# Batch 6's second column maximum, the store and reading back of its maxima and the load of its a, sooner in a pinned order

## The chip, the cores and the metric

The kernel runs on one core of one Trainium2 chip. The metric is device time in microseconds; the figure of a kernel is the median of its runs, and lower is better.

## What is computed

Slot attention over 8 batches and 8 heads (576 positions, head size 64, 32 slots), then a feed-forward block with GELU on the 4608 rows of 512 that come out of it.

```python
a = phi - np.max(phi, axis=2, keepdims=True)
a = np.exp(a)
a = a / (np.sum(a, axis=2, keepdims=True) + 1e-09)
k_m = np.einsum('bhsm,bhsd->bhmd', a, k)
v_m = np.einsum('bhsm,bhsd->bhmd', a, v)
scores = scale * np.matmul(q, k_m.transpose(0, 1, 3, 2))
...
attn = np.exp(scores)
...
attn = np.matmul(attn, v_m)
...
h = x @ w_in
g = 0.5 * h * (1.0 + erf(h * inv_sqrt2))
return (g @ w_out)
```

The softmax of `phi` runs over the 576 positions, one maximum for each of the 8 x 32 columns of a batch.

## The kernel before

The work is cut into batches 0 to 7. For each batch the kernel makes `a` (from `phi`), pools `k` and `v` with it into 32 slots per head, takes scores of `q` against the slots, and multiplies the attention with `U`, which holds the slots already multiplied with `w_in`. So TensorE does per batch: `h` (line 901, attention times `U`), GELU on ScalarE, and the product with `w_out` (line 941). Each float32 product is made of three products of high and low parts: `gh` and `gl` are the two parts of the GELU's result.

A piece of work is named in a string, START, as `name.batch.part`, and the pieces are recorded in the order in which they stand there. Every engine, and SyncE's queue of transfers, then takes its own instructions strictly in that order. Pieces after the string's end are put by a second, planned list that is the same in both kernels. Near the end of START batch 3 is in its feed-forward steps and batches 5 and 6 are being prepared. Names that matter here:

- `h.3.x.0`, `gelu.3.x.0`, `gh.3.0.i`, `gl.3.0.i`, `P.3.0.i`: batch 3, first half of the positions: `h` for block x of 128 hidden columns, its GELU (lines 913 and 915), the high part and the low part for blocks 2i and 2i+1 (lines 244 and 928), and their 12 products with `w_out` (line 941). The steps `h.3.14.0` to `P.3.0.7` and the second half `h.3.x.1` come from the planned list.
- `Lphi.6.g`, `amax.6.g`, `mw.6`, `mr.6`: batch 6's `phi`, transposed, in two halves g; the negated maximum of each half's columns, on VectorE (line 426, into `nm`); the store of these maxima to a small buffer in DRAM (`row<-nm`, line 480); and their reading back, spread over all partitions (`cols<-row`, line 485).
- `Lphin.6`: the load of batch 6's `phi` in its other layout into the tile `aT` (lines 468 and 473). `aadd.6`: VectorE subtracts the maxima there (lines 516 and 520, `aT<-aT,cols`). `ax.6`: ScalarE's exponential of it (line 509). `aexp.6.g`: the exponential of the transposed half with its sum (line 432). The tiles `aT`, `cols` and `phi` have one buffer each.
- `slots.5`, `slots.6`: TensorE's pooling (lines 536 and 549), which reads `aT` and the `kv` tiles. `km.5`: the scaled result (line 581). `Lkv.6.g.c`: the ten loads of batch 6's k and v. `Lq.4`: three loads of q for batch 4, read by `score.4` (line 619, `psc<-q,kT`). `Lphi.7`: the next `phi`, into the same buffer.

`aadd.6` stands between `gl.3.0.5` and `gh.3.0.6` on VectorE, and `aexp.6`, `ax.6` between the GELUs of blocks 13 and 14 on ScalarE; both come from the planned list.

```python
def a_out(b):
    row = st["row", b] = dram.tile([P, G], F32, tag="row", name=f"row_{b}")
    nc.sync.dma_start(row, col("nm", b))
```

Of the kernel before, what the change touches and what calls it, by code (L numbers as in the profile page):

```python
# [137 lines left out]
h.3.0.0 gh.2.1.6 gelu.2.15.1 gl.2.1.6 h.3.1.0 P.2.1.5 P.2.1.6 gh.2.1.7:a gelu.3.1.0 gelu.3.0.0  # L138
h.3.2.0 gh.3.0.0 gl.2.1.7 h.3.3.0 gl.3.0.0 gelu.3.2.0 slotsT.4 Up.3.12.4 kT.4 gelu.3.3.0
Up.3.8.4 P.2.1.7 O.2.1.0:a h.3.4.0 O.2.1.1 Uh.3.12 P.3.0.0 Lkv.5.0.0 Uh.3.8 gh.3.0.1:a  # L140
gelu.3.4.0 gl.3.0.1 h.3.5.0 amax.6.0 h.3.6.0 gelu.3.5.0 gh.3.0.2:a h.3.7.0 gl.3.0.2 P.3.0.1
gelu.3.7.0 Ul.3.8 gelu.3.6.0 h.3.8.0 h.3.9.0 gelu.3.8.0 gh.3.0.3:a P.3.0.2 gl.3.0.3 aadd.5
pT.3.1 P.3.0.3 ax.5 amax.6.1 gelu.3.9.0 gh.3.0.4 slots.5.0 ph.3.1:d slots.5.1 Lkv.6.1.1
Lkv.6.1.4 km.5.0 Lkv.6.0.0 pl.3.1 Lkv.6.0.4 gl.3.0.4 Lphin.6 Ul.3.12 Lkv.6.0.2 mw.6 km.5.1
mr.6 Lkv.6.0.1 Lkv.6.1.3 Lkv.6.0.3 Lkv.6.1.2 Lkv.6.1.0
"""


# [1126 lines left out]
```

## Time and profile before

| | |
|---|---|
| median of 3 runs | 709.08 us (708.46 to 712.72) |
| profiled execution | 708.37 us |
| its span | 706.6 us |
| TensorE matmul busy | 686.3 us, 97% of the span |
| VectorE busy | 372.2 us, 53% |
| ScalarE busy | 306.2 us, 43% |
| mean granted TensorE clock | 0.985 |

The span is what the profiler's rows cover; 1.8 us of the execution's own time lie around it. Times in rows are microseconds from the span's start. PE is TensorE's matmul, DVE VectorE, ACT ScalarE, SPq SyncE's queue of transfers.

### The profile page before, as it was taken

To read this page: it belongs to the slowest core of one execution; us is meant where nothing else is said; L and a number is where in the kernel's file an instruction comes from. 1 tells how busy PE (TensorE), PEld (TensorE's weight loads), DVE (VectorE), ACT (ScalarE), POOL (GpSimd) and SP (SyncE) were. 2 spreads that over 40 slices of the span, in tenths; PEclk is the share of its full clock that TensorE was granted. 3 is DMA by queue.
4 is the path that set the end of the run, shared out by engine and by line. 5 is a ranking of instruction groups with operands and counts; after the bars stand their busy time and mean duration, and the time that the engine had idled before them with its cause. 6 is when DMAs were issued, how large, how long until landed. Compare 5 with 4: busy or idle time off the path is not lost.

```text
span 706.6 us, 12344 instructions
## 1 busy us (share of the span) xinstructions
PE 686.3 (97%) x4942; PEld 569.4 (81%) x4942; DVE 372.2 (53%) x689; ACT 306.2 (43%) x789; POOL 45.2 (6%) x38
## 2 busy tenths in 40 slices
PE   6799999999999999997999999999999999999997
PEld 5577888888768888885887888888887888788886
DVE  3989878855672634243944346432834346432222
ACT  5879668345452373443543225322521315322220
POOL 1333143300000000000000000000000000000000
PEclk9799999999999999998999999999999999999999
DMA  9973255412248161135600200020000200000001
GB/s 335 375 271 120 94 214 134 156 56 85 98 135 227 60 163 62 45 95 183 205 0 31 83 2 31 1 97 1 31 1 31 83 1 31 1 31 0 31 1 45
DMA packets 30717, 64.37 MB, mean 91 GB/s; under 512 B 3780, under 2 KB 8644, under 8 KB 30660
## 3 DMA queue, kind: packets, MB, share of 16 engines
q1 hardware_dynamic: 30564, 63.46, 26.9%
q8 instruction: 39, 0.64, 0.4%
q10 hardware_dynamic: 96, 0.13, 0.1%
q14 instruction: 18, 0.15, 0.1%
HBM read 54.13 MB, written 9.44 MB: 90 GB/s over the span
## 4 chain that ended last, share of the span: by engine, by line
PE 90%; DMA 6%; ACT 2%; DVE 1%; SPq 1%; issue 0%; POOL 0%; ACTq 0%
PE acc L941 49%; PE h L901 27%; PE tacc L941 6%; PE pu L619 4%; DMA raw<-w_out 2%; DMA raw<-w_in 1%; PE psc L619 1%; DMA kv<-kv 1%; PE psc L536 1%; DMA row<-nm 1%; DMA cols<-row 1%; PE x L536 1%; ACT phi L432 0%; PE pk L536 0%; SPq L288 0%
## 5 line engine op out<-in xcount | busy, mean ns | idle before, releaser
L941 PE MATMUL acc<-wo_hi,gh 128*128 128x512 f32 x512 | 202.0, 395 | 5.2 <-DVE gh L244 5.2
L901 PE MATMUL h<-p_hi,U 128*128 128x288 f32 x1024 | 201.6, 297 | 0.2 <-ACT tails L922 0.2
L941 PE MATMUL acc<-wo_hi,gl 128*128 128x512 f32 x512 | 200.3, 391 | 0.0
L941 PE MATMUL acc<-wo_lo,gh 128*128 128x512 f32 x512 | 200.3, 391 | 0.0
L913 ACT ACTIVATE gf<-h 128x256 f32<-128x256 f32 x192 | 73.8, 387 | 253.8 <-issue 158.4
L901 PEld LDWEIGHTS h<-p_hi,U 128*128 128x128 f32 x1024 | 162.7, 188 | 19.5 <-issue 7.5
L244 DVE CAST gh<-gf 128x512 fp32r<-128x512 f32 x100 | 42.4, 424 | 177.1 <-ACT gf L913 156.4
L941 PEld LDWEIGHTS acc<-wo_hi,gh 128*128 128x128 f32 x512 | 96.9, 189 | 29.6 <-DVE gh L244 5.4
L941 PEld LDWEIGHTS acc<-wo_hi,gl 128*128 128x128 f32 x512 | 96.5, 188 | 21.7 <-DVE gl L928 1.3
L928 DVE TENSOR_TENSOR gl<-gf,gh 128x512 fp32r<-128x512 f32 x128 | 90.3, 708 | 38.9 <-ACT gh L244 31.2
L941 PEld LDWEIGHTS acc<-wo_lo,gh 128*128 128x128 f32 x512 | 96.6, 189 | 16.2
L901 PE MATMUL h<-p_lo,U 128*128 128x288 f32 x512 | 108.7, 294 | 0.0
L901 PEld LDWEIGHTS h<-p_lo,U 128*128 128x128 f32 x512 | 81.3, 188 | 0.5 <-DVE p_lo L739 0.5
L860 DVE TENSOR_TENSOR U<-pu,U 128x512 fp32r<-128x512 f32 (+2 forms) x50 | 40.7, 835 | 30.8 <-ACT U L244 30.5
L915 ACT ACTIVATE tails<-h 128x32 f32<-128x32 f32 x192 | 37.5, 195 | 0.0
L619 PE MATMUL pu<-w_in_sb,kT 64*32 64x512 f32 (+2 forms) x624 | 34.4, 528 | 1.4 <-POOL w_in_sb L342 0.8
L244 ACT CAST U<-pu 128x512 fp32r<-128x512 f32 (+2 forms) x43 | 28.8, 710 | 7.4 <-PE pu L619 6.2
L941 PE MATMUL tacc<-wo_hi,gh_t 128*128 128x512 f32 x64 | 25.3, 395 | 0.0
L941 PE MATMUL tacc<-wo_lo,gh_t 128*128 128x512 f32 x64 | 24.9, 389 | 0.0
L941 PE MATMUL tacc<-wo_hi,gl_t 128*128 128x512 f32 x64 | 24.9, 389 | 0.0
L309 ACT ACTIVATE y<-raw 128x512 f32<-128x512 f32 x28 | 19.0, 680 | 8.0 <-DMA raw<-w_out 3.3
L342 POOL TENSOR_TENSOR y<-y,raw 128x512 int32<-128x512 int32 x14 | 18.8, 1343 | 57.7 <-DVE raw L318 25.3
(126 smaller groups left out, 576.5 us busy)
## 6 DMA issues: line engine op xcount, KB each, us to landing
kv<-kv SPq DMA_DIRECT2D x48, 256.0 KB, 5.3
out<-o SPq DMA_DIRECT2D x16, 512.0 KB, 2.9
raw<-w_out SPq DMA_DIRECT2D x14, 512.0 KB, 8.5
raw<-w_in SPq DMA_DIRECT2D x14, 512.0 KB, 4.9
q<-qT SPq DMA_DIRECT2D x9, 576.0 KB, 4.9
phi<-phiT SPq DMA_DIRECT2D x16, 288.0 KB, 4.7
aT<-phiN SPq DMA_DIRECT2D x6, 512.0 KB, 4.8
q<-qT SPq DMA_DIRECT2D x10, 288.0 KB, 7.7
```

Of the source, the lines that this page charges most:

```text
L244: return e.copy(dst, src) if e is nc.scalar else e.tensor_copy(dst, src)
L309: nc.scalar.activation(y, high.bitcast(F32), AF.Abs, scale=2.0**16)
L342: nc.gpsimd.tensor_tensor(w, y, low, op=ALU.add)
L536: nc.tensor.matmul(pk[32 * j : 32 * j + 32, : 2 * D], st["aT", b][:, c, g, 32 * j : 32 * j + 32], st["kv", b, g, c][:, :, j, :], start=(c ...
L619: nc.tensor.matmul(ps[g][M * j : M * j + M], st["kT", b][rows, t, M * j : M * j + M], moving[j][rows], start=True, stop=True,)
L860: nc.vector.tensor_sub(u[:, ..., 1, :], pu, u[:, ..., 0, :].bitcast(F32))
L901: i = nc.tensor.matmul(h[:, :HS], u[g][w], x[:, g, :], start=(n == 0), stop=(n == 3 * G - 1))
L913: nc.scalar.activation(gf[:, f % 2 * n : f % 2 * n + n], h[:, :n], AF.Gelu)
L915: nc.scalar.activation(t, h[:, n:HS], AF.Gelu)
L928: nc.vector.tensor_tensor(g_of("gl", *k), g_of("gf", *k), g_of("gh", *k).bitcast(F32), op=ALU.subtract)
L941: nc.tensor.matmul(acc, x, w[:, f, :], start=(first and n == 0), stop=(last and n == 2))
```

## The change

Three pieces of batch 6 move ahead in START, and nothing else does: `amax.6.1` and `mw.6` to right behind `amax.6.0`, `mr.6` to behind `ax.5`, and `Lphin.6` to ahead of `Lkv.6.1.1`. No instruction is added or taken away.

```diff
-gelu.3.4.0 gl.3.0.1 h.3.5.0 amax.6.0 h.3.6.0 gelu.3.5.0 gh.3.0.2:a h.3.7.0 gl.3.0.2 P.3.0.1
...
+gelu.3.4.0 gl.3.0.1 h.3.5.0 amax.6.0 amax.6.1 mw.6 h.3.6.0 gelu.3.5.0 gh.3.0.2:a h.3.7.0
...
+gl.3.0.3 aadd.5 pT.3.1 P.3.0.3 ax.5 mr.6 gelu.3.9.0 gh.3.0.4 slots.5.0 ph.3.1:d slots.5.1
+Lphin.6 Lkv.6.1.1 Lkv.6.1.4 km.5.0 Lkv.6.0.0 pl.3.1 Lkv.6.0.4 gl.3.0.4 Ul.3.12 Lkv.6.0.2
```

On SyncE's queue, around the loads of batch 6 (`row` and `cols` are `mw.6` and `mr.6`, `aT` is `Lphin.6`, `kv` and `kvw` are `Lkv.6`, the first line is a store of batch 2's output), the kernel before has:

```order
L980 DMA out<-o_1_3330 128x2x512
L382 DMA kv_0_0_3357<-kv 128x512
L382 DMA kv_1_1_3513<-kv 128x512
L372 DMA kvw_3515<-kv 64x512
L382 DMA kv_0_0_3519<-kv 128x512
L372 DMA kvw_3515<-kv 64x512
L468 DMA aT_3526<-phiN 128x4x256
L473 DMA aT_3526<-phiN 128x1x128
L382 DMA kv_0_2_3531<-kv 128x512
L480 DMA row_3533<-nm_3374 128x2
L485 DMA cols_3536<-row_3533 128x256
L382 DMA kv_0_1_3538<-kv 128x512
```

The same place of the queue in the changed kernel:

```order
L980 DMA out<-o_1_3330 128x2x512
L382 DMA kv_0_0_3357<-kv 128x512
L480 DMA row_3377<-nm_3374 128x2
L485 DMA cols_3468<-row_3377 128x256
L468 DMA aT_3517<-phiN 128x4x256
L473 DMA aT_3517<-phiN 128x1x128
L382 DMA kv_1_1_3520<-kv 128x512
L372 DMA kvw_3522<-kv 64x512
L382 DMA kv_0_0_3526<-kv 128x512
L372 DMA kvw_3522<-kv 64x512
L382 DMA kv_0_2_3535<-kv 128x512
L382 DMA kv_0_1_3538<-kv 128x512
```

The store and the reading back now stand ahead of all ten loads of batch 6, with the two `aT` loads right behind them; the five loads that stood ahead of the store stand behind.

On VectorE, from `gl.3.0.1` to `gh.3.0.4` (`nm` is the maximum, `aT` and `cols` here are batch 5's `aadd`), the kernel before has:

```order
L928 TENSOR_TENSOR gl_0_1_3365<-gf_0_1_3286,gh_0_1_3360 128x512
L426 TENSOR_REDUCE nm_3374<-phi_3021 128x1
L928 TENSOR_TENSOR gl_0_2_3394<-gf_0_2_3362,gh_0_2_3385 128x512
L860 TENSOR_TENSOR U_2_3317<-pu_8_3308,U_2_3317 128x2x512
L928 TENSOR_TENSOR gl_0_3_3445<-gf_0_3_3408,gh_0_3_3431 128x512
L516 TENSOR_TENSOR aT_3054<-aT_3054,cols_2950 128x1024
L520 TENSOR_TENSOR aT_3054<-aT_3054,cols_2950 64x128 x2
L802 STREAM_TRANSPOSE pT_1_3450<-sT_1_2751 128x576
L426 TENSOR_REDUCE nm_3374<-phi_3021 128x1
L244 CAST gh_0_4_3468<-gf_0_4_3428 128x512
```

And in the changed kernel:

```order
L928 TENSOR_TENSOR gl_0_1_3365<-gf_0_1_3286,gh_0_1_3360 128x512
L426 TENSOR_REDUCE nm_3374<-phi_3021 128x1 x2
L928 TENSOR_TENSOR gl_0_2_3397<-gf_0_2_3362,gh_0_2_3388 128x512
L860 TENSOR_TENSOR U_2_3317<-pu_8_3308,U_2_3317 128x2x512
L928 TENSOR_TENSOR gl_0_3_3448<-gf_0_3_3411,gh_0_3_3434 128x512
L516 TENSOR_TENSOR aT_3054<-aT_3054,cols_2950 128x1024
L520 TENSOR_TENSOR aT_3054<-aT_3054,cols_2950 64x128 x2
L802 STREAM_TRANSPOSE pT_1_3453<-sT_1_2751 128x576
L244 CAST gh_0_4_3472<-gf_0_4_3431 128x512
```

The second maximum has left its place behind batch 5's transpose and follows the first. The order on TensorE, ScalarE and GpSimd is the same in both kernels.

## Rows read from the trace of the kernel before

**Rows 1.** TensorE's waits from 60 us on: us in total, times, longest us.

```profile
PE acc L941 <- DVE gh L244: 5.2, 1, 5.2
PE h L901 <- ACT tails L922: 0.2, 1, 0.2
```

**Rows 2.** The chain that ended last, 283 to 345 us: start, us, what.

```profile
313.21 5.14 DMA row<-nm
...
318.37 5.04 DMA cols<-row
```

**Rows 3.** Timeline of SyncE's queue of transfers, 285 to 345 us: start, us, what.

```profile
293.26 16.41 SPq L382 DMA_DIRECT2D kv<-kv  x2
...
318.73 3.89 SPq L382 DMA_DIRECT2D kv<-kv  x5
322.67 0.43 SPq L413 DMA_DIRECT2D q<-qT  x1
...
324.16 1.03 SPq L358 DMA_DIRECT2D phi<-phiT  x2
```

**Rows 4.** VectorE's timeline; in brackets the idle time before, and what ended it.

```profile
295.84 0.75 DVE L426 TENSOR_REDUCE nm<-phi 128x1 f32<-128x576 f32 x1
297.58 0.69 DVE L928 TENSOR_TENSOR gl<-gf,gh 128x512 fp32r<-128x512 f32 x1 [0.99 <-ACT gh L244]
...
304.39 0.60 DVE L520 TENSOR_TENSOR aT<-aT,cols 64x128 f32<-64x128 f32 x2
...
305.72 0.71 DVE L426 TENSOR_REDUCE nm<-phi 128x1 f32<-128x576 f32 x1
...
323.43 1.23 DVE L516 TENSOR_TENSOR aT<-aT,cols 128x1024 f32<-128x1024 f32 x1 [9.09 <-DMA cols<-row]
...
325.19 0.43 DVE L244 CAST gh<-gf 128x512 fp32r<-128x512 f32 x1
...
330.60 1.47 DVE L426 TENSOR_REDUCE nm<-phi 128x1 f32<-128x576 f32 x2 [0.93 <-DMA phi<-phiT]
```

**Rows 5.** TensorE's timeline around the wait.

```profile
309.64 0.45 PE L549 MATMUL x<-kvw,aT 64*32 64x128 f32 x16
...
314.48 0.42 PE L901 MATMUL h<-p_hi,U 128*128 128x288 f32 x2
...
316.06 0.39 PE L941 MATMUL acc<-wo_hi,gh 128*128 128x512 f32 x1
...
318.77 0.42 PE L901 MATMUL h<-p_hi,U 128*128 128x288 f32 x2
...
325.67 0.80 PE L941 MATMUL acc<-wo_hi,gh 128*128 128x512 f32 x1 [5.16 <-DVE gh L244]
...
330.44 0.42 PE L901 MATMUL h<-p_hi,U 128*128 128x288 f32 x2
...
331.31 1.20 PE L619 MATMUL psc<-q,kT 64*32 64x288 f32 x32
```

**Rows 6.** Busy us by stretch, the last three: granted clock, DMA share, GB/s.

```profile
325.00:330.00 5.00, 4.33 (x11) 3.31 (x12) 2.64 (x7) 3.28 (x6) 0.00 (x0) 0.52 1.04 400
```

**Rows 7.** ScalarE's timeline from batch 6's exponentials on.

```profile
319.48 0.19 ACT L432 ACTIVATION_READ_ACCUMULATOR phi<-phi,nm 128x1 f32 x1
325.19 1.16 ACT L509 ACTIVATE aT<-aT 128x1152 f32<-128x1152 f32 x1 [5.52 <-DVE aT L520]
326.37 1.28 ACT L913 ACT_TABLE_LOAD   x1
327.67 0.38 ACT L913 ACTIVATE gf<-h 128x256 f32<-128x256 f32 x1
327.95 0.19 ACT L915 ACTIVATE tails<-h 128x32 f32<-128x32 f32 x1
```

**Rows 8.** The page's transfers: engine, count, KB each, median us from issue to landing.

```profile
q<-qT SPq DMA_DIRECT2D x9, 576.0 KB, 4.9
...
aT<-phiN SPq DMA_DIRECT2D x6, 512.0 KB, 4.8
q<-qT SPq DMA_DIRECT2D x10, 288.0 KB, 7.7
```

More of the change, by code (lines that the diff above doesn't have):

```diff
@@ L140 @@
 Up.3.8.4 P.2.1.7 O.2.1.0:a h.3.4.0 O.2.1.1 Uh.3.12 P.3.0.0 Lkv.5.0.0 Uh.3.8 gh.3.0.1:a
-gelu.3.4.0 gl.3.0.1 h.3.5.0 amax.6.0 h.3.6.0 gelu.3.5.0 gh.3.0.2:a h.3.7.0 gl.3.0.2 P.3.0.1
[L142 to L145, printed above, removed]
+gelu.3.4.0 gl.3.0.1 h.3.5.0 amax.6.0 amax.6.1 mw.6 h.3.6.0 gelu.3.5.0 gh.3.0.2:a h.3.7.0
+gl.3.0.2 P.3.0.1 gelu.3.7.0 Ul.3.8 gelu.3.6.0 h.3.8.0 h.3.9.0 gelu.3.8.0 gh.3.0.3:a P.3.0.2
+gl.3.0.3 aadd.5 pT.3.1 P.3.0.3 ax.5 mr.6 gelu.3.9.0 gh.3.0.4 slots.5.0 ph.3.1:d slots.5.1
+Lphin.6 Lkv.6.1.1 Lkv.6.1.4 km.5.0 Lkv.6.0.0 pl.3.1 Lkv.6.0.4 gl.3.0.4 Ul.3.12 Lkv.6.0.2
+km.5.1 Lkv.6.0.1 Lkv.6.1.3 Lkv.6.0.3 Lkv.6.1.2 Lkv.6.1.0
 """
```

## The prediction

> **What bounds the kernel now.** TensorE is busy for 97% of the span, so I first asked where it is not. The list of its waits from 60 us on has two rows, and only one is worth a step: 5.2 us, once, at the products with `w_out`, for VectorE's `gh` [rows 1]. Everything else on TensorE is work. TensorE's timeline puts that wait ahead of P.3.0.6, at 325.67 [rows 5]. Next I read the chain of waits backwards from there. It leaves TensorE for two transfers in a row, `row<-nm` (5.14 us from 313.21) and `cols<-row` (5.04 us from 318.37) [rows 2]. VectorE's timeline says the same from its side: it stood idle for 9.09 us before batch 6's `aadd` at 323.43, until `cols` had landed, and `gh`, queued behind it, could start only at 325.19 [rows 4]. So a small piece of batch 6's preparation holds up batch 3 because VectorE takes its work in order.
>
> Why was the store only issued at 313.21? Its data were there after 305.72 + 0.71 = 306.4 [rows 4]. SyncE's queue was blocked: the row of two loads that spans 16.41 us, from 293.26 to 309.67, is the last `kv` load of batch 5 and then the first of batch 6, which waits for the pooling of batch 5; and another six transfers stood between that one and `row` [rows 3].
>
> **What the wait costs.** A step runs `h`, products, `h`. In the step ahead, `h` to products is 316.06 - 314.48 = 1.58 us and products to the next `h` 318.77 - 316.06 = 2.71 [rows 5]. Without the wait P.3.0.6 would start at 318.77 + 1.58 = 320.35 and the next `h` at 323.06. That `h` started at 330.44 [rows 5], so the place costs 7.38 us: 5.32 of waiting and 330.44 - 325.67 - 2.71 = 2.06 because the 12 products ran slowly. The second part is TensorE's clock: the granted clock is 0.52 of full over 325 to 330, so nearly all of it at the lower of the two levels, 1.2 GHz, after 5 us in which TensorE did nothing [rows 6]. If the wait goes, both parts go.
>
> **The maxima, moved.** The first of batch 6's two maxima runs at 295.84 for 0.75 us; VectorE then sits idle for 0.99 us until 297.58, waiting for ScalarE [rows 4]. The second (0.71 us) fits into that gap and ends at about 297.3, so `gl.3.0.2` is not delayed. Cost nothing; without the gap it would be 0.7 us on VectorE alone. The other half of `phi` had to be there already: the first maximum shows no wait for it, and both halves were loaded together. The place left at 305.72 gives back 0.7 us of VectorE that nobody waits for.
>
> **The store and the reading back, moved.** On SyncE's queue `row` follows the last `kv` load of batch 5, issued at 293.26 [rows 3], so it goes out at about 297.3 and lands at 297.3 + 5.14 = 302.4. `cols` has one buffer, which batch 5's `aadd` reads until 304.39 + 0.60 = 305.0 [rows 4]; SyncE stands at it until then, and it lands at about 305.0 + 5.04 = 310.1. What is queued behind it on SyncE is `aT` and batch 6's `kv`; all of these wait for the pooling of batch 5, which ends at 309.64 + 0.45 = 310.1 [rows 5], or, for the first `kv` load, for a part of it that ended at about 309.2, so the new wait holds up nobody. It would start to when `row` took some 12 us instead of 5.
>
> **The load of a, moved.** It too has one buffer, free when that pooling ends: issue at 310.1, landing 4.8 us later [rows 8], 314.9. So `aadd.6` no longer waits for `cols` but for `aT`, from 314.9 on. It took 325.19 - 323.43 = 1.76 us up to `gh` [rows 4]: `gh.3.0.6` starts at about 316.7 and is done near 317.2, against 320.35 when TensorE wants it. Slack 3.2 us. Half of `kv` now stands behind `aT` and goes out about 2 us later than before, the other half sooner, as SyncE no longer stands at `cols` until 318.37 [rows 2].
>
> **What is late next.** TensorE comes 7.38 us sooner to everything behind the wait, and three things there do not all move as far.
>
> First, ScalarE. The `h` at 323.06 writes into a bank that the GELU of block 14 must have read. ScalarE ends `aexp.6` at 319.48 + 0.19 = 319.67 in both kernels; then come `ax.6`, a table load and that GELU, whose last part ended 327.95 + 0.19 - 325.19 = 2.95 us after `ax` began [rows 7]. Now `ax` need not wait (`aadd.6` is done by 316.7), so this ends at 322.62: 0.44 us before TensorE needs it. Cost nothing, but thin.
>
> The row shows the GELU 327.67 - 326.37 = 1.30 us after the start of the table load [rows 7]. The Trainium skill, page "ScalarE: Activation LUTs", section "What ACT_TABLE_LOAD costs", puts a switch at 1283 ns for the load plus about 1380 ns of drain. By that page the GELU would end 1.38 us later, TensorE would wait for 0.9 us and the gain would be 6.4 us, an estimate; the row shows the 1.28 us alone, so the sum goes by the row.
>
> Second, q of batch 4. `score.4` starts 331.31 - 330.44 = 0.87 us behind that `h` [rows 5], now at 323.93, and its second half needs the 288 KB loads some 0.3 to 0.6 us on. Before, `q` was issued at 322.67, behind five `kv` loads from 318.73 on, 0.78 us each [rows 3]. Now these five come right behind `aT` and four shorter runs of issues. From 310.1, seven issues at about 0.55 us reach the first of the five at 314.0, and at 0.55 to 0.78 each `q` is issued at 316.8 to 317.9, its halves by 318.8. With the 4.9 us of its row [rows 8] it lands at 321.7 to 322.8, in time; the halves, with the 7.7 us of theirs, would land as late as 326.5 and TensorE would wait up to 2.2 us. I lean to the first end: before, the last halves were issued near 323.6 and were used by 331.9 without any wait, beside a `phi` load that landed at 330.6 though it was issued at 324.16 [rows 3, 4], 6.4 us with all of q ahead of it at 400 GB/s [rows 6]; here only what stands ahead of q counts. Bytes lean the same way: 2.9 MB of `aT` and `kv` and 1.15 MB of q, moving from 311 on, are through by 321 at the 400 GB/s of that row, and by 324.4 at 300. Taken as nothing, range 0 to 2.2 us.
>
> Third, `phi` of batch 7. Its buffer is free at 319.67, so it goes out at 319.7 instead of 324.16 [rows 3], 4.5 us sooner and not 7.4; its maxima, which began at 330.60 after a wait of 0.93 us [rows 4], move to about 326. What stands behind them on VectorE is the transposes of `score.4`, which wait for work of TensorE that now ends near 328. Cost nothing. `kv` and `ax` of batch 6, needed by TensorE at about 325, are there by 321.
>
> **The sum.** The profiled execution took 708.37 us, 706.6 of it span. 708.37 - 7.38 = 701.0. The runs of the kernel before lie 0.1 to 0.7 us above that profiled one in the two lower of three, so I put the median at **701.4**.
>
> **Rivals.** (a) q is late: TensorE gets past P.3.0.6 but waits at `score.4`. The order leaves q behind twelve loads, which speaks for it; the landing of q without a wait before speaks against it. Gain 7.38 less 0.4 to 2.2: 701.8 to 703.6, middle 702.7. (b) `aT` is late: if it lands after 318.1, `gh` (1.76 us on, 0.43 long) misses 320.35, and each us beyond costs one. That would take 8.0 us instead of 4.8; the longest landing in these rows is 7.7 [rows 8]. About 702.3. (c) ScalarE comes back to GELU late: each us beyond the 0.44 costs one. One more stretch as long as the table load's row, 1.28 us [rows 7], would cost 0.84: 701.9 on the sum below. The drain that the Trainium skill's page states would be such a stretch. (d) The wait stays as long as it was, because something other than `cols` and `aT` releases `gh` late: 708.4 to 709. The bracket in VectorE's row names `cols`, and `gh` follows `aadd` at once, so this is weak. (e) Slower: SyncE stands at `cols` for `row`, and everything of batch 6 is queued behind it. `aT` would have to be issued at 318.6, not 310.1, to bring `aadd.6` back to 323.43, which needs `row` to land at about 318, 20.8 us after its issue, four times the 5.14 us of its row [rows 2]. From there each us costs one; at 24 us it gives 711.6.
>
> **How the numbers follow.** Forecast 0.72, (a) 0.17, (b) 0.04, (c) 0.03, (d) 0.02, (e) 0.02. The forecast alone covers 700.6 to 702.0; with (a) and most of (b) and (c) the range is 700.6 to 703.6. A measurement of this kernel tells about 1% from no change, 7.1 us here, and the gain that I expect is only just above: 702.0 is the line. Of the forecast's 0.72 I put 0.58 beyond it, the rest stays inside with (a) to (d): faster 0.58, same 0.40, slower 0.02.
>
> **What would show it.** Right: the list of TensorE's waits from 60 us on has no `gh` row; `row<-nm` is issued near 297 and `cols<-row` near 305; `aadd.6` waits for `aT` and starts near 315; ten `kv` loads run through without a break; the clock stays at 1.00 around 320 to 330; P.3.0.6 starts at about 320.4. Wrong: a new wait of TensorE at `psc<-q,kT` near 324 (a), or at `h` near 323 for ScalarE (c); `aadd.6` later than 318 (b); or, with all steps as said, a span that is shorter by much less than 7 us, since then something later must give it back.

## The result, and the profile after

The changed kernel takes 703.17 us, the median of 6 runs (702.47 to 705.19), against 708.89 us for the kernel before beside it, the median of 6 as well; one run of the latter, at 902.64, was disturbed and is left out of the ratio. The ratio is 0.9915, with a 95% interval of 0.9888 to 0.9943: 0.85% faster, inside the 1% that I had called no change (0.40, against 0.58 for faster). It lies in the predicted range of 700.6 to 703.6, in the case of rival (a) and not of the forecast. The interval lies wholly below 1, so the gain is real; the time is 1.8 us above the forecast's 701.4.

The profiled execution took 705.19 us, the slowest of its six; its span is 703.4. Part of that has nothing to do with the change: P.3.0.5, the step ahead of the wait [rows 5], already began 318.69 - 316.06 = 2.63 us later. Over all the traces of this case this head of the program lies between 315.60 and 318.78 us, though its work on TensorE is the same, and the delay arises in the first 60 us. So I measure the **place**: from the first product of P.3.0.5 to the first matmul of batch 6's pooling, `slots.6`. From that matmul to the span's end it is 374.2 us in this kernel and in the one before, and the head is noise. Where TensorE never waits, the place is 2.71 + 1.58 + 2.71 + 0.87 + 1.13 = 9.00 us: 12 products, `h`, 12 products, `h`, `score.4`. Before, it ended with this row of TensorE's timeline (the row behind the last of [rows 5]):

```profile
332.44 1.95 PE L536 MATMUL psc<-kv,aT 128*32 128x128 f32 x64
```

So it took 332.44 - 316.06 = 16.38 us, 7.38 over 9.00, which is the cost that the prediction put on the wait and its slow clock.

TensorE's waits of the changed kernel from 60 us on, as in [rows 1]:

```profile
PE psc L619 <- DMA q<-qT: 0.5, 1, 0.5
PE h L901 <- ACT tails L922: 0.2, 1, 0.2
```

The row for `gh` is gone; one for q is new. TensorE's timeline, as in [rows 5]:

```profile
318.69 0.39 PE L941 MATMUL acc<-wo_hi,gh 128*128 128x512 f32 x1
...
322.99 0.39 PE L941 MATMUL acc<-wo_hi,gh 128*128 128x512 f32 x1
...
325.70 0.42 PE L901 MATMUL h<-p_hi,U 128*128 128x288 f32 x2
...
327.11 2.18 PE L619 MATMUL psc<-q,kT 64*32 64x288 f32 x32 [0.46 <-DMA q<-qT]
329.22 1.95 PE L536 MATMUL psc<-kv,aT 128*32 128x128 f32 x64
```

P.3.0.6 (322.99) has no bracket: it follows its `h` at once. The place is 329.22 - 318.69 = 10.53 us, so 5.85 of the 7.38 us came back and 1.53 are left. They stand in the row of `score.4`: 0.46 ahead of it and 2.18 instead of 1.20 [rows 5] inside it. Only the wait ahead of a group has a bracket; one in its midst makes the group long, and the list of waits shows 0.5 of 1.5. The chain of waits names the cause, the last half of q:

```profile
323.42 5.14 DMA q<-qT
328.56 0.04 issue
328.60 0.69 PE psc L619 x8
```

VectorE's timeline, as in [rows 4]: the two maxima together, the low part behind them, `aadd.6` in its two parts, `gh.3.0.6`, and batch 7's maxima.

```profile
298.48 1.41 DVE L426 TENSOR_REDUCE nm<-phi 128x1 f32<-128x576 f32 x2
300.22 0.69 DVE L928 TENSOR_TENSOR gl<-gf,gh 128x512 fp32r<-128x512 f32 x1 [0.33 <-ACT gh L244]
...
316.89 1.22 DVE L516 TENSOR_TENSOR aT<-aT,cols 128x1024 f32<-128x1024 f32 x1
319.51 0.59 DVE L520 TENSOR_TENSOR aT<-aT,cols 64x128 f32<-64x128 f32 x2 [1.40 <-DMA aT<-phiN]
320.13 0.43 DVE L244 CAST gh<-gf 128x512 fp32r<-128x512 f32 x1
...
329.28 1.41 DVE L426 TENSOR_REDUCE nm<-phi 128x1 f32<-128x576 f32 x2 [2.60 <-DMA phi<-phiT]
```

SyncE's queue, as in [rows 3]:

```profile
299.91 0.33 SPq L480 DMA_DIRECT2D row<-nm  x1
307.65 0.33 SPq L485 DMA_DIRECT2D cols<-row  x1
312.88 0.38 SPq L468 DMA_DIRECT2D aT<-phiN  x1
313.31 0.56 SPq L473 DMA_DIRECT2D aT<-phiN  x1
...
316.19 5.30 SPq L382 DMA_DIRECT2D kv<-kv  x6
321.54 0.43 SPq L413 DMA_DIRECT2D q<-qT  x1
322.19 1.58 SPq L419 DMA_DIRECT2D q<-qT  x2
323.88 0.84 SPq L358 DMA_DIRECT2D phi<-phiT  x2
```

The six `kv` loads that took 5.30 us were not issued without a break: in the list of what this queue waited for, 313 to 324 us (us in total, times, longest), a `kv` load stands for the landing of `aT`, which it doesn't read, and two more for earlier loads of k and v.

```profile
SPq L382 <- DMA aT<-phiN: 1.8, 1, 1.8
SPq L382 <- DMA kv<-kv: 0.6, 1, 0.6
SPq L382 <- DMA kvw<-kv: 0.4, 1, 0.4
```

(The 3.3 us that the expectation of a_back names are the sum over 295 to 345 us; 1.5 of them are batch 7's loads.) Each of these three names the transfer eight places ahead of the load that waits: the small load of `aT`, then the next two, `kv` and `kvw`. So the transfers seem to take eight completion semaphores in turn; that is read off these waits and was not tried. The small load of `aT` (64 KB, issued at 313.31) landed only near 319.5, when the second part of `aadd.6` started: some 6.2 us, while the 512 KB load issued before it was there by 316.89.

### The profile page after: what moved, and what is told of

The parts are those of the page before. It is cut to its first block, busy times and chain, and to the rows that moved or that the text cites. A ratio compares the mean times of both kernels' runs of the same rounds, so it can differ in the third digit from the quotient of the medians.

```text
span 703.4 us, 12344 instructions
## 1 busy us (share of the span) xinstructions
PE 686.9 (98%) x4942; PEld 568.9 (81%) x4942; DVE 373.0 (53%) x689; ACT 306.1 (44%) x789; POOL 45.2 (6%) x38
## 3 DMA queue, kind: packets, MB, share of 16 engines
HBM read 54.13 MB, written 9.44 MB: 90 GB/s over the span
## 4 chain that ended last, share of the span: by engine, by line
PE 92%; DMA 3%; ACT 2%; DVE 2%; issue 0%; POOL 0%; SPq 0%; ACTq 0%
PE acc L941 49%; PE h L901 28%; PE tacc L941 6%; PE pu L619 5%; DMA raw<-w_out 1%; PE psc L619 1%; PE psc L536 1%; DMA q<-qT 1%; DMA phi<-phiT 1%; PE x L536 1%; ACT phi L432 0%; PE pk L561 0%; ACT L432 0%; PE pt L457 0%; DVE y L314 0%
## 5 line engine op out<-in xcount | busy, mean ns | idle before, releaser
L342 POOL TENSOR_TENSOR w_in_sb<-y,raw 128x512 int32<-128x512 int32 x14 | 20.4, 1465 | 29.8 <-DVE raw L318 7.9
```

The source lines that it names most:

```text
L342: nc.gpsimd.tensor_tensor(w, y, low, op=ALU.add)
```

## The experiments

Each kernel was timed beside the kernel before on the same chip; the medians of the latter were 708.89 to 710.66. Two questions are open. Where the gain came from: my theory is that VectorE and SyncE take their work in order, and that the sooner store lets `aadd.6` go sooner. And what makes q late, for the rest of 1.53 us: its late issue on SyncE, the bytes ahead of it, or one transfer that holds it up. The places, with 9.00 as the least, are each read from one profiled execution:

| kernel | place, us | median (range, runs), us | ratio to before (95%) |
|---|---|---|---|
| before | 16.38 | 708.89 | |
| changed | 10.53 | 703.17 (702.47 to 705.19, 6) | 0.9915 (0.9888 to 0.9943) |
| changed, again | 10.11 | 703.43 (702.65 to 704.82, 4) | 0.9916 (0.9885 to 0.9947) |
| changed, third time | 10.90 | 703.84 (1) | |
| q_ahead | 9.01 | 701.42 (701.01 to 703.36, 4) | 0.9885 (0.9867 to 0.9902) |
| a_back | 9.19 | 702.01 (701.92 to 702.14, 4) | 0.9888 (0.9873 to 0.9903) |
| store_only | 10.97 | 703.77 (703.56 to 704.77, 4) | 0.9915 (0.9901 to 0.9930) |
| load_a_only | 18.36 | 710.66 (1) | |
| aadd_behind_gh | 16.22 | 709.69 (707.44 to 711.23, 10) | 0.9987 (0.9969 to 1.0005) |
| swap_a | 9.94 | 703.46 (702.09 to 704.06, 4) | 0.9917 (0.9891 to 0.9944) |
| half_kv | 10.26 | 702.09 (1) | |
| split_a | 10.28 | 702.89 (702.22 to 703.69, 4) | 0.9908 (0.9891 to 0.9924) |
| no_phi7 | 10.39 | 702.62 (1) | |
| half_and_split | 9.02 | 700.66 (1) | |

### Which order makes the wait: aadd_behind_gh

On the kernel before, `aadd.6` behind `gh.3.0.6` instead of ahead of it:

```diff
-    put(108, "aadd.6")
+    put(109, "aadd.6")
```

> The kernel before, order of the string unchanged, with only batch 6's subtraction taken one piece later on VectorE, behind the high and low part for P.3.0.6. Theory (two engines that work in order stand at the late maxima): P.3.0.6 no longer waits, but ScalarE still stands at batch 6's exponential until the subtraction, so the next h waits about 5 us for GELU of block 14, and TensorE's clock falls after it: 15 to 16 on the measure (16.38 before), time 0.5 to 1.5 us below before. Rival (VectorE's order alone was the trouble): 9 to 10.5, time 6 to 7 us below before.

The time stayed, 709.69 us. TensorE's wait is as long as before, but stands one step later, at the `h` behind P.3.0.6:

```profile
329.19 0.85 PE L901 MATMUL h<-p_hi,U 128*128 128x288 f32 x2 [5.21 <-ACT tails L915]
```

`cols` was as late as ever; VectorE no longer blocked `gh`, but ScalarE, in order too, stood at `ax.6` for the same `aadd.6`, and the GELU that frees the bank for `h` is queued behind `ax.6`. So it was not VectorE's order alone, and a cure that leaves both engines' order has to make `cols` land sooner. The place came out a little above the expected 15 to 16.

### The parts of the change: store_only, a_back, load_a_only

`store_only`, on the kernel before: only the second maximum and the store stand early.

```diff
-gelu.3.4.0 gl.3.0.1 h.3.5.0 amax.6.0 h.3.6.0 ...
+gelu.3.4.0 gl.3.0.1 h.3.5.0 amax.6.0 amax.6.1 mw.6 h.3.6.0 ...
-... Lkv.6.0.2 mw.6 km.5.1
+... Lkv.6.0.2 km.5.1
```

> The kernel before with the second maximum and the store early, the reading back and the load of a at their old places. Theory: the 7.4 us came from the chain of two transfers that began at the late store; with the store early alone the reading back is issued at its old turn, about 313.2 on the clock of the kernel before, lands at 318.3, and the subtraction starts 5.1 us sooner than 323.4: P.3.0.6 waits 0 to 0.3 us, q is out at 317 to 318, so 9.0 to 10 on the measure (16.38 before, 10.53 changed). Rival (the reading back and the load of a had to move too): 12 to 16.4.

The place is 10.97, so these two pieces alone give 5.41 of the 7.38, and the expected 9 to 10 was missed. `cols` was issued right behind the loads at 313.78, but took 6.35 us, and VectorE still stood for it, TensorE too. VectorE's and TensorE's timelines:

```profile
320.15 1.23 DVE L516 TENSOR_TENSOR aT<-aT,cols 128x1024 f32<-128x1024 f32 x1 [5.24 <-DMA cols<-row]
```

```profile
322.38 0.50 PE L941 MATMUL acc<-wo_hi,gh 128*128 128x512 f32 x1 [1.29 <-DVE gh L244]
```

q did not wait here: `score.4` took its 1.20 us. After the wait of 1.29, P.3.0.6 began slowly (0.50 us for its first product), which makes up the 1.97 over 9.00.

`a_back`, on the changed kernel: the load of a goes back to its old place behind four loads of `kv`, so that the store and the reading back alone are early.

```diff
-Lphin.6 Lkv.6.1.1 Lkv.6.1.4 km.5.0 Lkv.6.0.0 pl.3.1 Lkv.6.0.4 gl.3.0.4 Ul.3.12 Lkv.6.0.2
+Lkv.6.1.1 Lkv.6.1.4 km.5.0 Lkv.6.0.0 pl.3.1 Lkv.6.0.4 gl.3.0.4 Lphin.6 Ul.3.12 Lkv.6.0.2
```

> The changed kernel with the load of a back at its old place, behind four of batch 6's k and v loads; maximum, store and reading back stay early. The bytes ahead of q are the same and start 0.9 us sooner. Theory of issue (q is late since SyncE stood for the landing of the load of a, the eighth transfer back, 3.3 us in all): with that load further back SyncE issues q about 2 us sooner than the changed kernel, the wait at the scores goes, 9.0 to 9.3 on the measure that is 10.53 changed; 701.6 to 702. Rival, theory of bytes (the engines are full until q is through): q lands at most 0.9 us sooner, 9.6 to 10.2; 702.3 to 702.9. Rival, the load of a is now late itself: a wait at P.3.0.6, more than 10.5.

The place is 9.19, nearly the least: `score.4` took 1.38 us, 0.18 more than without a wait. P.3.0.5 starts at 316.78 here; SyncE's queue and then TensorE:

```profile
310.06 0.33 SPq L382 DMA_DIRECT2D kv<-kv  x1
...
313.41 2.87 SPq L382 DMA_DIRECT2D kv<-kv  x6
316.95 0.33 SPq L413 DMA_DIRECT2D q<-qT  x1
```

```profile
324.66 1.38 PE L619 MATMUL psc<-q,kT 64*32 64x288 f32 x32
325.97 1.95 PE L536 MATMUL psc<-kv,aT 128*32 128x128 f32 x64
```

The first `kv` load starts 316.78 - 310.06 = 6.72 us ahead of P.3.0.5, while in the changed kernel the first load of the batch, `aT`, starts 318.69 - 312.88 = 5.81 ahead: `aT` has to wait for the end of batch 5's pooling, the first `kv` load only for a part of it. The six `kv` loads run through in 2.87 us instead of 5.30, and q is issued 0.17 us after P.3.0.5 begins instead of 2.85. The issue theory's numbers were met, but SyncE still stood for `aT`, 0.7 us at q and 1.4 us ahead of its halves; the edit moved that behind the `kv` loads, started the loads 0.9 us sooner and put the small load further back, and which of these counted is not shown. So the third move of the change, the load of a, took back 10.53 - 9.19 = 1.3 us of what the other two gave (0.9 to 1.7 with the further executions of the changed kernel, below); the runs of the two kernels don't overlap.

`load_a_only`, on the kernel before: that third move by itself.

```diff
-... slots.5.1 Lkv.6.1.1
-... gl.3.0.4 Lphin.6 Ul.3.12 Lkv.6.0.2 mw.6 km.5.1
+... slots.5.1 Lphin.6 Lkv.6.1.1
+... gl.3.0.4 Ul.3.12 Lkv.6.0.2 mw.6 km.5.1
```

> The kernel before with only the load of a moved ahead of batch 6's k and v loads; maximum, store and reading back at their old places. Theory: the subtraction waits for the reading back as before, so no gain: 16.2 to 16.6 on the measure (16.38 before). Rival (the load of a was part of what held the subtraction): below 15.5.

A miss, and by 2 us: the place is 18.36 (its one time can't be told from before). I had expected no effect, since `aadd.6` waited for `cols` and not for `aT`. But `row` and `cols` are queued behind the loads, `row` went out at 314.39 and took 5.96 us, and `cols` at 320.37. VectorE:

```profile
325.62 1.23 DVE L516 TENSOR_TENSOR aT<-aT,cols 128x1024 f32<-128x1024 f32 x1 [11.01 <-DMA cols<-row]
```

### Is q's place in the queue enough: q_ahead

On the changed kernel, q's first load stands behind the store and its halves among the first loads of `kv`; the `kv` loads that they pass go out later.

```diff
-... amax.6.0 amax.6.1 mw.6 h.3.6.0 ...
+... amax.6.0 amax.6.1 mw.6 Lq.4.0 h.3.6.0 ...
-... km.5.0 Lkv.6.0.0 pl.3.1 Lkv.6.0.4 ...
+... km.5.0 Lkv.6.0.0 pl.3.1 Lq.4.1 Lkv.6.0.4 ...
```

> The changed kernel with batch 4's q loads put ahead of most of batch 6's k and v loads: the first right behind the store of the maxima, the two halves behind the third k and v load. Measure: us from the first product of P.3.0.5 to the first matmul of batch 6's pooling; 16.38 before, 10.53 changed, 9.00 if TensorE never waits. Theory (the 1.5 us left are q landing late, and nothing else): no wait at the scores, 9.0 to 9.2, time 1.5 us below the changed kernel, near 701.6. Rival 1 (batch 6's k and v are just as late as q, so the wait moves on to the pooling): 10 to 10.6, time 702.5 to 703.2. Rival 2 (ScalarE's return to GELU or the maxima of batch 7 hold TensorE as well): a wait at h, 9.5 or more.

The place is 9.01 and TensorE's list of waits has no q any more. Its median of 701.42 us is below those of both kernels, and it is the forecast's 701.4. SyncE's queue, the halves of q, and TensorE:

```profile
315.26 1.06 SPq L419 DMA_DIRECT2D q<-qT  x2
```

```profile
326.25 1.20 PE L619 MATMUL psc<-q,kT 64*32 64x288 f32 x32
327.38 1.96 PE L536 MATMUL psc<-kv,aT 128*32 128x128 f32 x64
```

Only q moved, and the whole rest went: the 1.53 us are q's and nothing else's. The wait for `gh` and the one for q together make all of the 7.38.

### Why q is late: after_again, after_third, swap_a, half_kv, split_a, no_phi7, half_and_split

The changed kernel itself, twice more, for its spread:

> The changed kernel once more, beside the next one. Measure as before (first product of P.3.0.5 to the first matmul of batch 6's pooling). If the span is only head + this stretch + tail: 10.4 to 10.7 on the measure again, whatever the time of P.3.0.5's start, and 374.2 us from the pooling to the end. If the stretch itself varies from run to run: off by 0.5 us or more.

> The changed kernel a third time, beside the last: 10.1 to 10.6 on the measure if the two looks so far (10.53, 10.11) show its spread.

Its places are 10.11, 10.53 and 10.90, outside what I expected both times, by little. In that order, the last half of q was issued 4.31, 4.73 and 3.46 us after the start of P.3.0.5 and landed 9.44, 9.87 and 10.24 after it. A sooner issue did not mean a sooner landing: in the third execution it was issued first and landed last, after 6.78 us instead of 5.14. An effect on the place below 0.8 us can't be told from this spread.

`swap_a`: batch 6's small load of `aT` is issued ahead of the large one, with the same bytes.

> The changed kernel with the two loads of batch 6's a in the other order, the small one (64 KB) first. Same transfers, same bytes ahead of q. Theory of issue: in the changed kernel SyncE stood longest for the landing of the small one, 6.2 us after its issue, before it could issue its eighth successor; put first it lands sooner, and q is issued 1 us or more sooner: 9.2 to 10.1 on the measure (10.53 changed). Theory of bytes: 10.4 to 10.7.

A place of 9.94 and 703.46 us: not to be told from the spread. q was still late, its last half 9.28 us after P.3.0.5.

`half_kv`: batch 6's k and v are loaded by half, k alone, and the pooling takes k for v as well.

```diff
-        nc.sync.dma_start(t[:rows], kv[b, g, r : r + rows])
+        w = slice(0, 1 if b == 6 else 2); nc.sync.dma_start(t[:rows, w], kv[b, g, r : r + rows, w])
```

> The changed kernel with batch 6's ten k and v loads at half the bytes: only k is loaded, and the pooling of batch 6 uses k's values for v as well. Same number and order of transfers, 1.15 MB less ahead of q. Theory of bytes (the transfers' landings, and with them SyncE's turns, follow from what the engines have to move): SyncE hardly stands for landings, q is out 2 us or more sooner against the start of P.3.0.5, no wait at the scores, 9.0 to 9.2 on the measure (10.53 and 10.11 in two looks at the changed kernel). Theory of issue (a landing takes its 6 us whatever is moved beside it): 9.9 to 10.6.

The bytes theory falls as it stood: 1.15 MB less ahead of q, its last half issued 2.45 us after P.3.0.5 and so 1.0 to 2.3 us sooner, and it still landed 9.60 after it. It took 7.15 us (the chain of waits), and TensorE still waited for it:

```profile
318.34 7.15 DMA q<-qT
```

A row of windows (busy us of each engine, then granted clock, DMA share and GB/s) shows that little was moving while the last of q landed, at 325.49: 90 GB/s at 0.23 of the engines.

```profile
324.00:326.00 2.00, 1.77 (x32) 0.49 (x32) 0.00 (x0) 0.40 (x2) 0.00 (x0) 1.00 0.23 90
```

So a few of the 16 transfer engines seemed to lag behind the others, and a transfer has landed when its last part has. What could load a few engines more than others? The small load of `aT` was the suspect, since it takes 6.2 us for 64 KB. The Trainium skill, page "DMA: Bandwidth & Descriptors", section "Why a DMA increments its semaphore by 16 and not by 1", says that a hardware-queue transfer is split over the largest number up to 16 that divides the slowest dimension of both sides; this load reads with 2 there, so two engines would carry all of it. The trace agrees, by its count of packets in the changed kernel, 312.5 to 330 us:

```profile
DMA packets 2692, 4.74 MB, mean 271 GB/s; under 512 B 258, under 2 KB 898, under 8 KB 2690
```

The queue issues 17 loads there, whose data come in packets of 512 B and more. The packets under 512 B are 258 = 16 x 16 + 2: 16 for each of 16 loads and 2 for one, if each engine that takes part in a load adds one. In half_and_split (below), with two loads of 64 rows in place of the small one, 18 loads have 288 = 18 x 16 (309.4 to 326.5 us). The trace has no row for a single transfer engine, so that those two engines are the ones that lag is not seen.

`split_a`: the small load as two, one for each half of the heads, each with 64 rows as its slowest dimension.

```diff
-        nc.sync.dma_start(
-            aT[:, NT, 0], phiN[b, MAIN:].rearrange("s (g n) -> g s n", g=G)
-        )
+        if b == 6:
+            for g in range(G):
+                nc.sync.dma_start(
+                    aT[TL * g : TL * g + TL, NT, 0], phiN[b, MAIN:, P * g : P * g + P]
+                )
+            return
...
```

> The changed kernel with the small load of batch 6's a (64 KB, 128 pieces of 512 bytes whose outer dimension is 2) as two loads of 64 rows each; same bytes, one transfer more. Third theory (that load runs on a few of the 16 transfer engines, which then are behind with everything queued after it, so q, spread over all 16, lands with the slowest of them; the thin tail of traffic after q in the changed kernel, 145 to 51 GB/s at 0.37 to 0.13 of the engines, is theirs): both parts of a land within 4.5 us instead of 5.6 to 6.2, SyncE stands less, the tail goes, q is there in time, 9.0 to 9.4 on the measure (10.11 to 10.90 in three looks at the changed kernel); near 701.8. Theory of issue: one more issue of 0.5 us ahead of q, 10.3 to 11.

The theory falls too, alone: the place is 10.28. The load did land sooner: issued from 310.50 on, `aadd.6`'s second part used it at 315.21 without a wait, and the six `kv` loads took 2.96 us instead of 5.30. But the last half of q, issued 2.90 us after P.3.0.5, took 6.72. VectorE, the chain, and the windows, which now show the engines full at 400 GB/s until q is nearly there:

```profile
315.21 0.60 DVE L526 TENSOR_TENSOR aT<-aT,cols 64x128 f32<-64x128 f32 x2
```

```profile
318.78 6.72 DMA q<-qT
```

```profile
318.00:320.00 2.00, 2.00 (x15) 1.88 (x14) 0.33 (x2) 2.00 (x5) 0.00 (x0) 1.00 1.05 400
...
322.00:324.00 2.00, 1.83 (x11) 1.44 (x9) 1.12 (x2) 0.78 (x5) 0.00 (x0) 1.00 1.03 406
```

`no_phi7`: the load of batch 7's `phi`, which is issued behind q and moves beside it, is left out, and batch 6's is used in its stead.

> The changed kernel without the load of batch 7's phi (0.6 MB in two transfers, issued right behind q); batch 7 uses batch 6's phi instead. In six looks q's last half landed 9.3 to 10.2 us after the start of P.3.0.5, near the end of all traffic, whatever stood ahead of it. Fourth theory (transfers queued behind q share the engines with it, so q lands with them): without phi q lands 1 us or more sooner, at 8.9 or before, 9.0 to 9.5 on the measure (10.11 to 10.90 changed). Rival (each engine works off its queue in order, and q waits for the one that is furthest behind): lands at 9.3 to 10.2, 10.0 to 10.9 on the measure, and the thin tail of traffic stays.

It fell as well: 10.39, with 0.40 us of wait at `score.4`. Leaving out what is queued behind q did nothing by itself.

`half_and_split` does both edits, since each had left what the other took away: half the bytes with a thin tail, or no tail with all the bytes.

> The changed kernel with both edits that did nothing alone: batch 6's k and v loads at half the bytes (k's values used for v as well), and the small load of its a in two loads of 64 rows. Theory of two causes, each enough by itself (the 4 MB queued up to q at some 400 GB/s, and a few engines kept behind by the small load): with both gone q's last half lands by 8.5 us after the start of P.3.0.5, 9.0 to 9.3 on the measure. Rival (neither is a cause; something that none of these edits touched sets q's landing): it lands at 9.3 to 10.2 again, 10.0 to 10.9 on the measure, and the cause of the late landing stays open.

The place is 9.02, without a wait (TensorE):

```profile
323.49 1.20 PE L631 MATMUL psc<-q,kT 64*32 64x288 f32 x32
324.62 1.95 PE L548 MATMUL psc<-kv,aT 128*32 128x128 f32 x64
```

The issue does not explain it: the last half of q was issued 318.66 - 315.60 = 3.06 us after P.3.0.5, later than in half_kv (2.45) and split_a (2.90), and the halves took 4.6 us:

```profile
q<-qT SPq DMA_DIRECT2D x2, 288.0 KB, 4.6
```

So two things were each enough to keep q late, which is why each single cure did nothing that can be told from the spread: the bytes queued ahead of it, and the small load. It is one execution, and it also leaves out v and adds one transfer; that the small load makes some engines lag is inferred from the thin tail and its going, not seen engine by engine.

## Why the prediction was partly right

**The wait, and what it cost: right.** [rows 5] and [rows 6] gave 7.38 us. q_ahead's place of 9.01 is 7.37 below 16.38. The clock part is right too: over 320 to 325 the granted clock was 1.00 in the changed kernel, and P.3.0.6's products kept 0.39 us each, where the first took 0.80 before [rows 5].

**The three moved pieces: right**, after taking off the head's 2.63 us. The store was predicted at 297.3 and went out at 299.91 - 2.63 = 297.28; the reading back at 305.0, and went out at 305.02; `aT` at 310.1, 310.25. `aadd.6` began at 314.26 against 314.9, right behind `gl.3.0.5` and without the wait for `aT` that I expected, but its second part waited 1.40 us for the small load, so `gh` began at 317.50 and not 316.7; the slack of 3.2 us took it. The 0.99 us of idle VectorE paid for the second maximum: 0.33 is left of it.

**What is late next, first (ScalarE): right.** GELU of block 14 ended at 325.15 - 2.63 = 322.52 against 322.62, and the `h` behind it started at 323.07 without a wait:

```profile
322.21 1.16 ACT L509 ACTIVATE aT<-aT 128x1152 f32<-128x1152 f32 x1
323.38 1.28 ACT L913 ACT_TABLE_LOAD   x1
324.68 0.39 ACT L913 ACTIVATE gf<-h 128x256 f32<-128x256 f32 x1
324.96 0.19 ACT L915 ACTIVATE tails<-h 128x32 f32<-128x32 f32 x1
```

From the table load's start to the GELU is 1.30 us again. The drain of 1.38 us that the Trainium skill's page "ScalarE: Activation LUTs" adds, in "What ACT_TABLE_LOAD costs", is not seen in either kernel.

**What is late next, second (q of batch 4): the step that failed.** The prediction took this wait "as nothing, range 0 to 2.2 us"; it measured 1.53 us, and 1.1 to 1.9 over three executions. The mechanism was named, as rival (a), and its price was right; the choice between its ends was wrong, on both of the reasons given. First, the issue: q was put at 316.8 to 317.9 and its halves by 318.8, and they came at 318.91 and, the last, 320.79. I had let ten `kv` loads "run through without a break", but SyncE stood 1.8 us for the landing of the small `aT` load and 1.0 us for `kv` and `kvw`. Second, the bytes: I took 400 GB/s for all from 311 on. What q had to wait for, 4032 KB (4.13 MB, where I counted 4.05), needed from 313.63 (311 with the head's 2.63) to 328.56, that is 277 GB/s on average, below even the 300 of the worse case, for which I had 324.4 (landed: 325.93). By stretches, with the DMA share and GB/s last:

```profile
316.00:318.00 2.00, 2.00 (x13) 1.80 (x12) 1.97 (x3) 0.00 (x0) 0.00 (x0) 1.00 0.72 196
318.00:320.00 2.00, 2.00 (x13) 1.80 (x12) 0.58 (x3) 1.56 (x5) 0.00 (x0) 1.00 1.08 288
```

The queue moved 196 GB/s over 316 to 318, for the most part before SyncE stood (317.7 to 319.5), and then 288 with the engines counted as fully busy; why so little is not shown. The 400 of [rows 6] came from a stretch in which no `aT` was under way. The two rows for q gave 4.9 and 7.7 us [rows 8], and I set aside that of the halves; the last took 5.14, 5.13 and 6.78 us in the three executions, so neither row was right for all of them. In the first, there was room for about 3.6: `score.4` is due 7.87 us behind P.3.0.5, at 326.56, and wants the halves some 0.45 on, and the last was issued at 323.42. Issued as forecast, at 318.8 + 2.63 = 321.43, it would have had room for 5.6, enough for 5.14; but the third execution issued it 1.27 us sooner against P.3.0.5, and it took 6.78, so that a sooner issue alone had been enough is not shown.

**Third (batch 7's `phi`): right in kind.** It was issued at 321.25 rather than 319.7, for the same late queue, and its maxima began at 326.65, predicted about 326, after a wait that holds up nobody on TensorE.

**The sum.** 708.37 - 5.85 for the place gives 702.5, and the head of that execution cost 2.63 more: 705.15 against 705.19 measured. The medians, whose heads are mixed, differ by 5.7. Of rival (a)'s 701.8 to 703.6 the middle was 702.7; that rival should have had more than 0.17. A queue position behind twelve loads and a thin slack spoke for it; one landing without a wait, in a kernel that came 7 us later to its use, spoke against it, and that was no evidence for the new case. Rivals (b) to (e) did not happen; the 701.9 of (c) stands on the 701.0 of the profiled execution, and on the median's 701.4 it would be 702.2; load_a_only shows how a queue order can turn the sign, by the same two transfers as in (e).

## What to carry to other kernels

When a wait is taken away, list everything that the waiting engine wants in the next few microseconds and ask of each load how much sooner it is issued: what does not move by as much as the engine can be the next wait, and then it gives back what its slack does not cover. A load's landing is not a property of the load: reckon with the longest row of its size, not with the median of another, when it is queued behind megabytes, and move it ahead if its buffer is free, as q_ahead did here for the last 1.5 us. Undo a change piece by piece: here two of three moves gave 7.2 us and the third cost 1.3.

## What the runs showed of the hardware

- A small load can be slow and hold others up: 64 KB of `aT`, with 2 as its slowest dimension, landed in some 6.2 us beside a 512 KB load that was there at least 2.6 us sooner; as two loads of 32 KB, the later one issued at most 1.2 us after the first, it was there within 4.7 us.
- The transfer that frees a completion semaphore can be one that the waiting load has nothing to do with: 1.8 us of SyncE's time went to the landing of the small `aT` load ahead of a `kv` load, eight places behind it.
- The store of 1 KB of maxima took 5.04 to 5.96 us to land in the three traces that have it on the chain of waits, as long as loads of some hundred KB. Their reading back took 5.04 to 6.35 us in four; in the changed kernel, where it goes out while little else moves, the list of transfers has 2.9.
- The first 316 us of the program differed by up to 3.2 us from execution to execution, more than most effects here, all of it from the first 60 us. In the changed kernel TensorE had a mean granted clock of 0.68 in the first 20 us, against 0.89 before, and the loads moved 344 GB/s in the next 20, against 360; which of the two it is was not tried, and another execution with a first 20 us at 0.73 had a short head. Comparing from a fixed step on removed it.
